# First batch's tiles in the memory of weight steps 12 to 14, weight conversion through the wo ring, and the third batch's pooling tied to weight step 13

## The chip, the cores and the metric

The program runs on one core of one Trainium2 chip. The metric is the device time of one execution in microseconds (us). Before the change the median of three runs is 1892.75 us (1891.44 to 1893.3).

## The reference

What is computed, cut to what matters:

```python
k_p = k.reshape(B, H, Sp, 8, D).mean(axis=3)         # B, H, S, D = 8, 8, 576, 64; Sp = 72
v_p = v.reshape(B, H, Sp, 8, D).mean(axis=3)
attn = softmax(q @ k_p.T / 8)
x = (attn @ v_p)                                     # to (8, 576, 512)
h = x.T @ U @ V                                      # mixing over the 576 tokens, rank 32
u = x + h.T
x1 = u + relu(u @ w_ch1) @ w_ch2                     # 512 -> 2048 -> 512
u2 = x1 + real(fft2(x1))
y = u2 + relu(layernorm(u2) @ w2_ch1) @ w2_ch2
```

The weights, U and V come as float64 and are turned into float32 on the chip, from the two 32-bit words of each number. A product at full precision is made of products of a high part (float32 rounded to the matmul's short form) and a low part (the rest).

## The kernel before

**Weights.** The first layer's two matrices are cut into 16 steps of 128 hidden units. A step has two raw tiles of 512 KB, one for each matrix (`wraw`, loaded at L167 on the SP queue). `w_first` (L159) is the generator that converts a step: `high` makes the top bits in ScalarE (L144, or VectorE at L146 when its last argument is false) and the scaled high word in ScalarE (L147), `bits` joins them with two VectorE operations (L151, L152) into a temporary, and `split` (L107) writes the high part in ScalarE (L108) and the low part in GpSimd (L102) into the weight tile `W[k, f]`. So a step is four operations of 128x512 each on VectorE, four plus two on ScalarE and two on GpSimd. The weight tile takes the memory of its own raw tile: both have the tag `w{k}_{f}`.

**Temporaries before.** The weight tiles' memory is lent out before a step's raw tile arrives: `scratch(i)` (L81) gives tile `w{i % 2}_{15 - i // 2}`. The first batch lives there: five tiles with its queries and its attention output (`xq`, `x0`, scratch 12 to 16, that is the memory of steps 9, 8 and 7), its raw keys and values (scratch 2 to 10), U and V (17 to 19), a table of U (`usf`, scratch 21: step 5), and temporaries of its softmax. A step's raw tiles can be loaded when the lent tile is given back. The conversion's own temporaries are scratch 0 and 1 (the memory of step 15) for steps 0 to 13, one tile for each step in turn, and the two `cv` buffers for steps 14 and 15.

**Attention.** `tile_steps` (L461) does one tile of 128 queries: scores on TensorE, row maxima on VectorE (L486), exponentials on ScalarE (L489), transposes, and the product with the pooled values, scaled by VectorE (L509). `first` (L522) runs the five tiles of batch 0, three at a time, as urgent work; `mix_split` and `mix_mm` (L546, L553) then add the mixing over the tokens, and `block_prep` (L802) transposes and splits the first two blocks of 256 tokens into `utx`. `prep` (L387) loads and pools the keys and values of a batch with nine VectorE reductions (L411, L414) through two `raw` buffers.

**The matmuls of the first layer.** In group 0 blocks 0 and 1 go together through the 16 steps: `st1` (24 matmuls of 256 columns, `h<-utx,w`), then ReLU in ScalarE (L998) and the low part in VectorE (L999), then `st2` (12 matmuls of 512 columns). Later groups take one block each, and the second half of the layer goes through products of combined weights, which `w_combine` (L199) makes: it adds and subtracts converted weights in VectorE through five `wo` buffers and stores them to DRAM. `w_second` (L244) does the second layer's weights through `cv` and `wo`.

**Order.** The program is written as lanes of generators that are stepped in turn. A planner orders each engine's instructions by their place in the program (urgent ones first) and by when its own clock holds them ready, so that late work can stand early in an engine's queue; each engine then runs its queue in that order. Buffers of one tag are handed out in the order of the program. The loads of all kinds share SP's queue.

The lines that gate the raw loads and choose the temporaries:

```python
            while len(raws) < min(NF, upto) and (len(raws) < (NF - 1 if state["free"] else 5) or NF - 2 in ts):
...
                if f < NF - 2:
                    t = scratch(f % 2)
                    t = [t[:, 512 * k:512 * k + 512].bitcast(I32) for k in range(2)]
                else:
                    t = [tmp().bitcast(I32) for k in range(2)]
```

Of the kernel before, what the change touches and what calls it, by code (L numbers as in the profile page):

```python
# [40 lines left out]
NRING = 4  # L41
QAHEAD = 3
# [4 lines left out]
def kernel(  # L47
# [30 lines left out]
    W = {}  # L78
    state = {"n": 0, "free": False, "m": "s1", "u": 0, "slot": 0, "x1": 0, "u2": 0, "op": 0, "clock": 0, "busy": False, "late": None, "tick": 0, "banks": ("s0", "s1", "hu")}
# [79 lines left out]
    def w_first(tmp):  # L159
        raws, ts = {}, {}  # L160

        def loads(upto):
            while len(raws) < min(NF, upto) and (len(raws) < (NF - 1 if state["free"] else 5) or NF - 2 in ts):
                f = len(raws)
                raws[f] = [wp.tile([128, 1024], I32, tag=f"w{k}_{f}", name="wraw") for k in range(2)]
                for k in range(2):
                    nc.sync.dma_start(out=raws[f][k], in_=(w1a, w2a)[k][f].bitcast(I32))  # L167
        def done(f):
            for k in range(2):
                w = wp.tile([128, 2, 512], F32R, tag=f"w{k}_{f}", name="w")  # L170
                W[k, f] = w
                split(w[:, 0], w[:, 1], ts[f][k].bitcast(F32), nc.gpsimd)
        loads(2)
        yield
        for f in range(NF + 1):
            loads(f + 3)
            while len(raws) < min(NF, f + 1):
                yield
                loads(f + 3)
            if f == NF - 1:  # L180
                done(f - 1)
            if f < NF:
                if f < NF - 2:
                    t = scratch(f % 2)
                    t = [t[:, 512 * k:512 * k + 512].bitcast(I32) for k in range(2)]
                else:
                    t = [tmp().bitcast(I32) for k in range(2)]
                ts[f] = t
                for k in range(2):
                    high(raws[f][k], 512, t[k], True)  # L190
            yield
            if f and f != NF - 1:
                done(f - 1)
            if f < NF:
                for k in range(2):
                    bits(raws[f][k], 512, t[k])
                yield
# [132 lines left out]
    class Attn:  # L330
        def __init__(self, c):
# [6 lines left out]
            self.usf = scratch(21)[:, 0:20 * RANK].rearrange("p (t g r) -> p t g r", t=5, g=4)  # L338
# [7 lines left out]
            self.xq = [scratch(12 + t) for t in range(5)]  # L346
# [10 lines left out]
        def tmp(self):  # L357
            return self.p.tile([128, S], F32, tag="raw", name="raw", bufs=2)
# [28 lines left out]
        def prep(self, b):  # L387
# [3 lines left out]
            self.kp[b] = (kp, vp)  # L391

            def load(i):
                t = scratch(2 + i) if b == 0 else self.tmp()
                if i < 4:
                    nc.sync.dma_start(out=t[:, 0:S], in_=kT[b, i])
                else:
                    r0, n = TT[i - 4]
                    nc.sync.dma_start(out=t[:n, 0:512], in_=vr[b, r0:r0 + n, :])
                self.raw[i] = t  # L400
# [60 lines left out]
        def tile_steps(self, b, t, alt=0, before=None):  # L461
# [11 lines left out]
            if 5 * b + t + QAHEAD >= 5:  # L473
                self.q_load(5 * b + t + QAHEAD)
            if before:
                before()
            sf = scratch(3 + alt) if alt else self.s
# [17 lines left out]
            e = scratch(4 + 2 * alt, 640) if alt else p1.tile([128, 640], F32, tag="e", name="e")  # L495
# [635 lines left out]
    lanes["w"] = w_first(at.cv)  # L1131
# [4 lines left out]
    for _ in f:  # L1136
        step("uv")
        step("w")
    with urgent():
        at.mix_split(0)  # L1140
    step("w")
    lanes["prep"] = lane_prep(at)
# [17 lines left out]
    state["free"] = True  # L1160
    hq = []
# [295 lines left out]
```

## Time and profile before

| what | us |
|---|---|
| median of 3 runs | 1892.75 |
| the profiled execution, its own time | 1888.01 |
| span of the profiled execution | 1886.2 |
| TensorE busy in the span | 1821.1 (97%) |
| VectorE busy | 1039.7 (55%) |
| ScalarE busy | 715.7 (38%) |
| GpSimd busy | 194.8 (10%) |

How to read it: the span goes from the first to the last instruction, and all times below are counted from its start. An engine's busy share is an average over stages; TensorE is nearly always busy but in the first part of the span, so the table of stretches below says more than the shares. In a timeline row the bracket at the end is the idle time of the engine before the row and the instruction that ended it.

### The profile page before, as it was taken

How to read it: one execution, taken by the hardware profiler on the slowest of the kernel's cores; microseconds unless marked ns; L12 is line 12 of the kernel's file. 1: busy time of each engine (PE TensorE's matmuls, PEld its weight loads, DVE VectorE, ACT ScalarE, POOL GpSimd, SP SyncE). 2: the span in 40 equal slices, each digit the busy share in tenths (PEclk: the TensorE clock that was granted, in tenths of full speed). 3: DMA queues.
4: the chain of work that ended last, by engine and by line, in shares of the span. 5: the costliest groups of instructions: out<-in, count | busy, mean ns of one | idle time of the engine just before them, and what ended most of it. 6: DMA issues, size and time to landing. Idle time of an engine off the chain costs nothing.

```text
span 1886.2 us, 31833 instructions
## 1 busy us (share of the span) xinstructions
PE 1821.1 (97%) x11492; PEld 1634.8 (87%) x11492; DVE 1039.7 (55%) x2379; ACT 715.7 (38%) x2186; POOL 194.8 (10%) x341
## 2 busy tenths in 40 slices
PE   5789999999999999999999999999999999999999
PEld 3678888888989898899998889899999899989998
DVE  7774575656565544554456655555565444444332
ACT  7672444444434332433324332333333323232321
POOL 3440131222210000000010100000100000000000
PEclk9899999999999999999999999999999999999999
DMA  9754475758575524667677766666676674756563
GB/s 361 255 174 128 144 229 158 244 179 248 164 243 163 176 73 150 220 219 245 216 237 253 276 223 229 227 222 230 225 241 216 213 238 172 238 179 231 182 208 132
DMA packets 265789, 394.41 MB, mean 209 GB/s; under 512 B 61664, under 2 KB 92480, under 8 KB 265632
## 3 DMA queue, kind: packets, MB, share of 16 engines
q1 hardware_dynamic: 264704, 388.97, 62.3%
q0 software_dynamic: 928, 3.40, 0.5%
q8 instruction: 91, 1.49, 0.3%
q14 instruction: 66, 0.54, 0.1%
HBM read 312.73 MB, written 79.56 MB: 208 GB/s over the span
## 4 chain that ended last, share of the span: by engine, by line
PE 62%; DVE 2%; DMA 2%; issue 0%; ACT 0%; SPq 0%; DVEq 0%; ACTq 0%
PE h L112 27%; PE o L112 16%; PE m L112 7%; PE hu L112 7%; PE s L112 4%; PE s L889 1%; DMA w<-wd 0%; DMA R<-x1d 0%; DMA wr<-wc 0%; DMA out<-ur 0%; DMA ur<-u2d 0%; DMA wd<-cv 0%; DVE hl L1278 0%; DVE bs L865 0%; DVE ur L105 0%
## 5 line engine op out<-in xcount | busy, mean ns | idle before, releaser
L112 PEld LDWEIGHTS h<-x,wr 128*128 128x128 f32 x4032 | 527.6, 191 | 24.5 <-DVE side L105 0.8
L112 PE MATMUL h<-x,wr 128*128 128x256 f32 x4032 | 547.9, 284 | 0.2 <-DVE side L105 0.2
L112 PE MATMUL o<-w,hh 128*128 128x512 f32 x1440 | 417.4, 400 | 4.9 <-ACT hh L998 2.5
L112 PE MATMUL h<-utx,w 128*128 128x256 f32 (+1 forms) x2232 | 321.7, 289 | 9.2 <-DVE hl L999 3.8
L112 PEld LDWEIGHTS h<-utx,w 128*128 128x128 f32 x2232 | 301.2, 191 | 29.5 <-DVE hl L999 6.4
L112 PEld LDWEIGHTS o<-w,hh 128*128 128x128 f32 x1440 | 251.0, 190 | 43.5 <-ACT hh L998 5.6
L112 PE MATMUL o<-w,hl 128*128 128x512 f32 x720 | 239.1, 395 | 1.7 <-DVE hl L999 1.7
L105 DVE TENSOR_TENSOR side<-h,side 128x256 f32<-128x256 f32 x192 | 106.3, 554 | 137.8 <-PE h L112 136.9
L112 PEld LDWEIGHTS o<-w,hl 128*128 128x128 f32 x720 | 131.5, 189 | 25.4 <-DVE hl L999 2.1
L1272 ACT ACTIVATE hh<-side 128x256 fp32r<-128x256 f32 x192 | 100.0, 521 | 118.8 <-DVE side L105 112.5
L1272 ACT ACTIVATE hh<-h 128x256 fp32r<-128x256 f32 x96 | 36.8, 383 | 253.2 <-PE h L112 250.8
L1278 DVE SCALAR_TENSOR_TENSOR hl<-h,hh 128x256 fp32r<-128x256 f32 x96 | 40.7, 424 | 158.8 <-ACT hh L1272 158.8
L1278 DVE SCALAR_TENSOR_TENSOR hl<-side,hh 128x256 fp32r<-128x256 f32 x192 | 105.9, 551 | 28.2 <-ACT hh L1272 28.1
L489 ACT ACTIVATE s<-s,mx 128x72 f32<-128x72 f32 x296 | 90.6, 334 | 58.5 <-DVE mx L486 57.5
L112 PE MATMUL m<-w,hh 128*128 128x512 f32 x400 | 109.8, 395 | 0.0
L112 PE MATMUL hu<-w,hh 128*128 128x512 f32 x384 | 104.8, 394 | 0.0
L102 POOL TENSOR_TENSOR wo<-wo 128x256 fp32r<-128x256 f32 x88 | 69.1, 801 | 289.6 <-ACT wo L108 242.8
L998 ACT ACTIVATE hh<-h 128x256 fp32r<-128x256 f32 x158 | 61.4, 389 | 80.5 <-PE h L112 77.8
L999 DVE SCALAR_TENSOR_TENSOR hl<-h,hh 128x256 fp32r<-128x256 f32 x158 | 65.7, 417 | 32.7 <-ACT hh L998 32.1
L102 DVE TENSOR_TENSOR x<-ul,x 128x256 fp32r<-128x256 f32 x154 | 59.3, 421 | 42.2 <-ACT x L108 42.0
L112 PEld LDWEIGHTS m<-w,hh 128*128 128x128 f32 x400 | 69.1, 190 | 9.2
L1317 ACT ACTIVATE side<-h 128x256 f32<-128x256 f32 x96 | 36.7, 383 | 99.4 <-PE h L112 99.4
(252 smaller groups left out, 2390.3 us busy)
## 6 DMA issues: line engine op xcount, KB each, us to landing
wr<-wc SPq DMA_DIRECT2D x336, 512.0 KB
wc<-wo SPq DMA_DIRECT2D x88, 256.0 KB
x<-x SPq DMA_DIRECT2D x56, 256.0 KB
ur<-ud SPq DMA_DIRECT2D x36, 256.0 KB
x1d<-ur SPq DMA_DIRECT2D x36, 256.0 KB
ul<-u2d SPq DMA_DIRECT2D x36, 256.0 KB
ur<-u2d SPq DMA_DIRECT2D x36, 256.0 KB
out<-ur SPq DMA_DIRECT2D x36, 256.0 KB
```

Source lines behind the costliest of these rows:

```text
L102: eng.tensor_tensor(out=o, in0=a, in1=b, op=ALU.subtract)
L105: eng.tensor_tensor(out=o, in0=a, in1=b, op=ALU.add)
L112: nc.tensor.matmul(o, a, b, start=start, stop=stop, skip_group_check=True)
L489: nc.scalar.activation(out=s[:n, a], in_=v[:, k], func=ACTF.Exp, bias=mx[:n, a:a + 1], accum_out=sm[:n, a:a + 1])
L889: nc.tensor.transpose(o[:, k * 128:k * 128 + 128], u[:, k * 128:k * 128 + 128], ident)
L998: nc.scalar.activation(out=hh, in_=p, func=ACTF.Relu)
L999: nc.vector.scalar_tensor_tensor(out=hl, in0=p, scalar=0.0, in1=hh.bitcast(F32), op0=ALU.max, op1=ALU.subtract)
L1272: nc.scalar.activation(out=hh[:, i], in_=c, func=ACTF.Relu)
L1278: nc.vector.scalar_tensor_tensor(out=hl[:, i], in0=c, scalar=0.0, in1=hh[:, i].bitcast(F32), op0=ALU.max, op1=ALU.subtract)
L1317: nc.scalar.activation(out=sb, in_=v, func=ACTF.Copy)
```

## The change

The first batch's five tiles move to scratch 2 to 6 (the memory of steps 14, 13 and 12), its raw keys and values to scratch 7 to 15, `usf` to scratch 16 (step 7), and the softmax's temporaries with them. Raw loads may run to step 11 once the first batch's attention is written, and to step 14 after the first two blocks are prepared. The conversion takes scratch 0 and 1 for steps 0, 1, 4, 5, 8 and 9, and two `wo` buffers each for the other ten steps; it no longer uses `cv`. For steps 0 to 4 the top bits of the first matrix are made in VectorE (L146's form) and no longer in ScalarE. The query loads of batch 1, which were written inside the urgent tiles of batch 0, are written after `mix_split(0)`, with no urgency. In `prep(2)` two small VectorE copies read a part of `W[1, 13]` and write into the tiles of the pooled keys and values.

```diff
+NSCR = 10
 ...
-            while len(raws) < min(NF, upto) and (len(raws) < (NF - 1 if state["free"] else 5) or NF - 2 in ts):
+            while len(raws) < min(NF, upto) and (len(raws) < state["most"] or NSCR + 1 in ts):
 ...
+        def temps(f):
+            if f < NSCR and f % 4 < 2:
+                t = scratch(f % 2)
+                return [t[:, 512 * k:512 * k + 512].bitcast(I32) for k in range(2)]
+            return [tmp().bitcast(I32).rearrange("p h x -> p (h x)") for k in range(2)]
 ...
-            if f == NF - 1:
-                done(f - 1)
             if f < NF:
 ...
-                ts[f] = t
+                ts[f] = temps(f)
                 for k in range(2):
-                    high(raws[f][k], 512, t[k], True)
+                    high(raws[f][k], 512, ts[f][k], k or f >= 5)
             yield
-            if f and f != NF - 1:
+            if f:
                 done(f - 1)
 ...
-            self.usf = scratch(21)[:, 0:20 * RANK].rearrange("p (t g r) -> p t g r", t=5, g=4)
+            self.usf = scratch(16)[:, 0:20 * RANK].rearrange("p (t g r) -> p t g r", t=5, g=4)
-            self.xq = [scratch(12 + t) for t in range(5)]
+            self.xq = [scratch(2 + t) for t in range(5)]
 ...
             self.kp[b] = (kp, vp)
+            if b == 2:
+                for z, i in ((kp, 4), (vp, 5)):
+                    nc.vector.tensor_copy(z[:, :, 0], W[1, NF - 3][:, 0, 0:i].bitcast(F32))
-                t = scratch(2 + i) if b == 0 else self.tmp()
+                t = scratch(7 + i) if b == 0 else self.tmp()
 ...
-            if 5 * b + t + QAHEAD >= 5:
+            if b:
                 self.q_load(5 * b + t + QAHEAD)
-            sf = scratch(3 + alt) if alt else self.s
+            sf = scratch(6 + alt) if alt else self.s
-            e = scratch(4 + 2 * alt, 640) if alt else p1.tile([128, 640], F32, tag="e", name="e")
+            e = scratch(8 + alt, 640) if alt else p1.tile([128, 640], F32, tag="e", name="e")
 ...
-    lanes["w"] = w_first(at.cv)
+    lanes["w"] = w_first(at.wo)
 ...
+    state["most"] = NF - 4
     with urgent():
         at.mix_split(0)
     step("w")
+    for i in range(QAHEAD):
+        at.q_load(5 + i)
 ...
     state["free"] = True
+    state["most"] = NF - 1
```

## Rows read from the trace of the kernel before

**Rows 1.** Busy time by stretch: us, PE, PEld, DVE, ACT, POOL, clock, DMA share, GB/s.

```profile
0.00:62.00 62.00, 31.34 (x146) 23.15 (x146) 50.98 (x95) 45.29 (x147) 23.55 (x36) 0.89 1.01 367
62.00:90.00 28.00, 26.03 (x158) 22.80 (x159) 18.39 (x32) 17.78 (x53) 10.40 (x10) 0.94 0.56 193
90.00:130.00 40.00, 33.69 (x202) 27.56 (x201) 36.19 (x58) 30.60 (x85) 20.80 (x16) 1.00 0.56 177
130.00:188.00 58.00, 54.94 (x353) 49.07 (x352) 25.14 (x51) 19.38 (x70) 4.37 (x7) 1.00 0.46 137
188.00:700.00 512.00, 497.78 (x3200) 449.73 (x3199) 306.34 (x712) 223.39 (x875) 80.82 (x113) 0.99 0.60 185
```

**Rows 2.** Timeline of TensorE, 40 to 68 us: start, duration, instruction, [idle before <-releaser].

```profile
44.87 1.97 PE L112 MATMUL hu<-scr,scr 128*128 128x512 f32 x2 [1.98 <-DVE scr L509]
...
55.19 1.12 PE L812 MATMUL s<-ident,scr 128*128 128x128 f32 x4 [2.67 <-DVE scr L105]
...
62.11 3.15 PE L112 MATMUL h<-utx,w 128*128 128x256 f32 x13 [3.19 <-DVE utx L102]
```

**Rows 3.** Timeline of TensorE, 85 to 130 us.

```profile
98.80 0.74 PE L112 MATMUL o<-w,hl 128*128 128x512 f32 x2 [1.67 <-DVE hl L999]
...
114.83 0.76 PE L112 MATMUL s<-k,q 128*128 128x144 f32 x4 [2.23 <-DVE x L509]
```

**Rows 4.** Timeline of VectorE, 93 to 122 us.

```profile
95.73 2.68 DVE L152 SCALAR_TENSOR_TENSOR scr<-wraw,scr 128x512 int32<-128x512 int32 x1
```

**Rows 5.** Timeline of all engines, 0 to 45 us.

```profile
0.74 1.56 SPq L442 DMA_DIRECT2D q<-qT  x3
...
13.81 2.29 PE L112 MATMUL s<-k,scr 128*128 128x144 f32 x8 [13.81 <-ACT k L421]
```

**Rows 6.** Groups of instructions, 13.8 to 62 us: busy us, mean ns.

```profile
L144 ACT ACTIVATE scr<-wraw 128x512 int32<-128x512 uint32 x13 | 8.8, 720 | 0.0
...
L105 DVE TENSOR_TENSOR wo<-w 128x256 f32<-128x256 f32 x6 | 3.4, 590 | 0.8 <-POOL w L102 0.8
...
L102 DVE TENSOR_TENSOR wo<-wo 128x256 f32<-128x256 f32 x4 | 2.7, 677 | 0.0
```

**Rows 7.** Line 146 over the whole span: ns min/median/max, first and last start.

```profile
L146 DVE TENSOR_SCALAR wo<-cv x32: 277/294/831, 293.6 to 516.7; 128x256 int32<-128x256 int32 x32
```

**Rows 8.** Timeline of VectorE, 41 to 62 us.

```profile
42.72 1.49 DVE L102 TENSOR_TENSOR wo<-wo 128x256 f32<-128x256 f32 x1
...
46.16 0.68 DVE L151 SCALAR_TENSOR_TENSOR scr<-wraw,scr 128x512 int32<-128x512 int32 x1
...
49.99 2.75 DVE L152 SCALAR_TENSOR_TENSOR scr<-wraw,scr 128x512 int32<-128x512 int32 x2
52.66 1.75 DVE L151 SCALAR_TENSOR_TENSOR cv<-wraw,cv 128x512 int32<-128x512 int32 x1
54.45 0.69 DVE L105 TENSOR_TENSOR scr<-o,scr 128x512 f32<-128x512 f32 x1
```

**Rows 9.** Timeline of GpSimd, 40 to 64 us.

```profile
49.22 6.32 POOL L102 TENSOR_TENSOR w<-scr,w 128x512 fp32r<-128x512 f32 x4 [3.87 <-DMA wc<-w]
...
63.04 1.48 POOL L102 TENSOR_TENSOR w<-cv,w 128x512 fp32r<-128x512 f32 x1 [0.83 <-ACT w L108]
```

**Rows 10.** Timeline of SP's queue, 116 to 140 us: first load of the second layer's weights.

```profile
131.56 0.64 SPq L248 DMA_DIRECT2D cv<-w1b  x1
```

**Rows 11.** Groups of instructions on VectorE, 90 to 130 us.

```profile
L414 DVE TENSOR_REDUCE vp<-raw 128x64 f32<-128x512 f32 (+1 forms) x8 | 5.3, 668 | 0.0
...
L411 DVE TENSOR_REDUCE kp<-raw 128x72 f32<-128x576 f32 x4 | 3.0, 738 | 0.0
```

**Rows 12.** Timelines of GpSimd, TensorE and ScalarE: last conversion, 16th step, batch 2's keys.

```profile
137.56 1.29 POOL L102 TENSOR_TENSOR w<-cv,w 128x512 fp32r<-128x512 f32 x1 [6.61 <-ACT w L108]
...
181.24 3.14 PE L112 MATMUL h<-utx,w 128*128 128x256 f32 x24
...
148.06 0.90 ACT L421 ACTIVATE k<-kp 64x288 f32<-64x288 f32 x2 [2.02 <-PE s L112]
```

More of the change, by code (lines that the diff above doesn't have):

```diff
@@ L78 @@
     W = {}
-    state = {"n": 0, "free": False, "m": "s1", "u": 0, "slot": 0, "x1": 0, "u2": 0, "op": 0, "clock": 0, "busy": False, "late": None, "tick": 0, "banks": ("s0", "s1", "hu")}
+    state = {"n": 0, "free": False, "m": "s1", "u": 0, "slot": 0, "x1": 0, "u2": 0, "op": 0, "clock": 0, "most": 5, "busy": False, "late": None, "tick": 0, "banks": ("s0", "s1", "hu")}
     def scratch(i, w=1024, dt=F32):
@@ L179, in w_first @@
                 loads(f + 3)
-            if f == NF - 1:
-                done(f - 1)
             if f < NF:
[L183 to L187, printed above, removed]
-                ts[f] = t
+                ts[f] = temps(f)
                 for k in range(2):
-                    high(raws[f][k], 512, t[k], True)
+                    high(raws[f][k], 512, ts[f][k], k or f >= 5)
             yield
-            if f and f != NF - 1:
+            if f:
                 done(f - 1)
@@ L195, in w_first @@
                 for k in range(2):
-                    bits(raws[f][k], 512, t[k])
+                    bits(raws[f][k], 512, ts[f][k])
                 yield
```

## The prediction

> **What bounds the kernel now.** I read the table of stretches first. From 188 us on TensorE is busy for 497.8 of 512 us, and for 54.9 of 58 us in the stretch before; up to 62 us it is busy for 31.3 us alone, and from 90 to 130 us for 33.7 of 40 [rows 1]. TensorE's work is not changed by this change, so what can be won is its idle time: 30.7 us before 62, 2.0 us from 62 to 90, 6.3 us from 90 to 130 and 3.1 us from 130 to 188. What is saved there moves all that follows forward, since TensorE stays the bound.
>
> Then the waits that open these gaps. Before the first matmul of the first layer (62.11 us) TensorE waits for VectorE again and again: 1.98, 2.67 and 3.19 us [rows 2]. From 90 to 130 us it is VectorE again, 1.67 and 2.23 us for a low part and for an attention tile [rows 3]. VectorE is busy for 51.0 of the first 62 us and for 36.2 of the 40 us [rows 1]. What stands before these late results in its queue is conversion: a joining step took 2.68 us at 95.73, and the low part that TensorE waited for came next [rows 4]. So the bound of both stretches is VectorE's queue, in order, with ScalarE close behind (45.3 of 62, 30.6 of 40 us).
>
> **The change part by part.** Durations are from the profiled execution, 1888.01 us, whose span is 1886.2 us; the median of the runs shown is 4.7 us above it, and I take the sum off the median. A minus is time saved.
>
> *Query loads.* Three loads of batch 1's queries stand first in SP's queue, for 1.56 us, ahead of the keys whose pooling the first matmul (13.81 us) waits for [rows 5]. They lose their urgency and go behind. The issue alone gives 1.6 us; as transfers they are 0.79 MB, 2.1 us at the 367 GB/s of that stretch [rows 1]. If V and U, on another queue, hold the keys back instead, little is left, say 0.5. I take -1.6, the time of the row itself. Their new place is behind the early raw loads; batch 1's first tile needs them only after the first layer has begun (62.11 us now), so no one waits there.
>
> *Top bits from ScalarE to VectorE.* One conversion takes 0.72 us on ScalarE [rows 6]. Five move; three belong to steps 0 to 2 and stand between the exponentials, so up to 2.2 us of ScalarE's part of the chain goes. The place may be filled by the next conversion; between 0 and -2.2 I take -1.0, a little under half. On VectorE the nearest row has 256 columns at 0.294 us [rows 7], so 512 are at most 0.59, five 2.9 us. Not all stand ahead of an urgent instruction: between 0 and +2.9 I take +1.2.
>
> *Temporaries in wo.* The ten VectorE operations of w_combine that the planner drew into this stretch cost 3.4 and 2.7 us, together 6.1 [rows 6]. One of them, 1.49 us long, stood directly before the result behind TensorE's 1.98 us wait [rows 2, 8]. The `wo` buffers now go to the steps' temporaries first, so the adds must come behind the conversion. That buffers are handed out in program order shows in `cv`: GpSimd was done with both buffers of step 14 at 64.52, yet the second layer's first load, which needs nothing else, was only issued at 131.56, after step 15 had had its turn [rows 9, 10]. Between -1.5 (that one) and -6.1 I take -3.0, since conversion fills a part of the room. Later the adds meet a VectorE that is busy for 306 of 512 us: no cost; without that slack their 6.1 us would come back.
>
> *Pooling of batch 2.* Of the rows from 90 to 130 us four reductions of keys (738 ns) and five of the eight of values (668 ns) are batch 2's, 6.3 us [rows 11]. They leave the crowded stretch for the time after step 13's conversion. TensorE idles 6.3 us in it, but most of a wait is a joining step, and one reduction stood ahead of about half the waits: between -0.7 (one reduction) and -6.3 I take -3.0. The two copies themselves are a few columns wide. They wait in VectorE's queue for step 13's high part, with low parts and row maxima queued behind: between 0 and 2 us (a wait like the largest in rows 3), I take +0.5.
>
> *Memory and ring.* Raw tiles of steps 5 to 11 may come earlier, those of 12 to 14 only once the first batch's tiles are stored, as 7 to 9 do now. The ring is two steps deeper. Neither is on TensorE's path now: the last conversion starts at 137.56 and the 16th step's matmuls at 181.24 [rows 12]. So I take 0, between -3 (the 2.0 and 1 us of small gaps from 62 to 90 and after 130) and +4: one more step's four joining steps, at the 0.68 us of the free case [rows 8] with GpSimd's collisions on top, ahead of the urgent chain.
>
> Sum: -1.6 - 1.0 + 1.2 - 3.0 - 3.0 + 0.5 + 0 = -6.9 us; 1892.75 - 6.9 = 1885.9 us. All low ends together give -20, all high ends +6.
>
> **Rule beside row.** While GpSimd's four subtractions ran from 49.22 to 55.54, three joining steps of 0.68 us took 2.75 and 1.75, so the urgent addition came at 54.45 and TensorE's next work at 55.19 [rows 2, 8, 9]. The Trainium skill (SBUF — State Buffer, "Who interferes with whom") says that a VectorE instruction with two SBUF inputs and a GpSimd instruction that reads SBUF exclude each other, and that the second waits for the whole of the first. By that rule the deeper ring is a danger, since it brings more subtractions beside joining steps into the early stretch; the rows above agree. What it could make of the time is the first rival's sum; with no further collisions the sum above stands.
>
> **The rivals.**
> 1. *Slower: conversion crowds the urgent chain (0.13).* Now the early conversion runs dry: a part of step 5's memory holds the table of U, which the sum that ends at 46.84 us still reads [rows 2]. With that memory free, two more steps could enter the queue from 44 to 62 us. That is eight joining steps, 5.4 us free, plus twice the 2.5 us that four subtractions cost (4.5 instead of 2.0): 10.4 us. If the stretch from 62 to 90 also idles like the next one (6.3 us in 40, so 4.4 in 28 instead of 2.0), 2.4 more. 12.8 - 6.9 gives +5.9, 1898.7 us. It decides from 10.7 us of delay on. For: the rows above. Against: VectorE is already full there, and the planner puts urgent work first.
> 2. *Absorbed (0.2).* ScalarE and VectorE stay full, freed room is refilled with conversion, and only the start's 1.6 us and one reduction's 0.7 remain: 1890.4 us. For: VectorE has no free room up to 62 us.
> 3. *All of it (0.2).* The adds' 6.1, the reductions' 6.3, the start's 1.6 and ScalarE's 2.2 come through whole: -16.2, 1876.6 us. For: each sat in a full in-order queue. Against: the longest waits were behind joining steps.
> 4. *The adds do not leave (0.06).* If w_combine still comes early, its term falls: -3.9, 1888.9 us. Against: the cv row.
> 5. *Batch 2 comes late (0.06).* Its keys are needed at 148.06 [rows 12]. If its pooling starts only with the last conversion at 137.6, nine reductions (6.3 us) and seven loads behind two buffers (256 KB at the 177 GB/s of rows 1, 1.5 us each) end near 154; a score matmul at the head of TensorE's queue would stand for 6 us: 6 - 6.9, 1891.9 us. Against: TensorE has first-layer work to 188.
>
> **How the numbers follow.** The forecast has 0.35, with a range of its own from 1882 to 1889. A measurement of this kernel can tell 0.2% from no change, that is 3.8 us: faster is below 1889.0, slower above 1896.5. Faster: most of the forecast (0.33), rival 3 (0.2), half of rival 4 and a quarter of rival 2 (0.08): 0.61. Slower: rival 1 and a little of 2 and 5: 0.15. Same: the rest, 0.24. The range reaches from rival 3 to beyond 2 and 5, 1875 to 1896; outside are rival 1 and the far ends.
>
> **What would show it.** In the new profile: the first matmul near 12.2 us instead of 13.8; the first layer's first matmul at 57 to 59 us instead of 62.1; no VectorE `wo<-w` before the last conversion; no pooling of batch 2 before step 13; TensorE's idle time from 90 to 130 us at about 3 us instead of 6.3. Wrong would be a first-layer start at 62 us or later, or VectorE waits in front of TensorE as long as now, with as many joining steps over 1 us.

## The result, and the profile after

The changed kernel takes 1902.76 us (median of 4 runs, 1900.58 to 1906.19), the kernel before 1892.1 us (4 runs) on the same chip: a ratio of 1.0051, 95% interval 1.0039 to 1.0063, so 10.7 us slower. I had forecast 1885.9 us, 6.9 us faster. The profiled execution of the changed kernel took 1900.69 us, its span is 1898.9 us. Lines of the code have moved down by one to three: the matmul helper is now L113, the top bits L145 and L147, the joining operations L152 and L153, the split L109 and L103.

The table of stretches of the changed kernel, with the columns of [rows 1]:

```profile
0.00:62.00 62.00, 35.31 (x159) 28.03 (x160) 52.44 (x93) 44.38 (x145) 26.51 (x38) 0.83 1.02 370
62.00:90.00 28.00, 22.31 (x127) 18.43 (x126) 21.57 (x36) 23.15 (x63) 14.67 (x12) 0.94 0.81 274
90.00:130.00 40.00, 31.01 (x170) 25.98 (x170) 33.74 (x55) 20.89 (x53) 16.42 (x13) 0.91 0.44 132
130.00:188.00 58.00, 56.43 (x365) 50.72 (x364) 24.09 (x49) 19.65 (x76) 2.13 (x5) 1.00 0.35 107
188.00:700.00 512.00, 493.23 (x3157) 442.92 (x3156) 304.00 (x711) 223.21 (x877) 81.27 (x113) 0.99 0.60 185
```

Read it against [rows 1]. From 62 to 90 us TensorE is busy for 22.31 us instead of 26.03, from 90 to 130 us for 31.01 instead of 33.69, and there the mean granted clock is 0.91 instead of 1.00. The conversion has run ahead: in 62 to 90 us ScalarE is busy for 23.15 instead of 17.78 us and the DMA moves 274 instead of 193 GB/s. Of the 64 joining operations of VectorE, 48 have started by 90 us, where 38 had before.

**Where the time went.** TensorE's work is the same, so a span is its work plus its idle time, plus what it loses at half clock. I counted, from the matmul and clock records, the idle time plus half of the time that TensorE was busy at half clock. What is left of the span is 1812.2 us before and 1813.0 us after, so this loss explains nearly all of the difference of the spans (12.7 us):

| loss of TensorE, us | 0 to 62 | 62 to 130 | 130 to 255 | 255 to 710 | after 710 | sum |
|---|---|---|---|---|---|---|
| before | 34.6 | 9.9 | 7.8 | 12.9 | 8.9 | 74.0 |
| changed | 33.9 | 19.5 | 7.6 | 16.1 | 8.9 | 85.9 |

So 9.6 us come from 62 to 130 us: 6.4 us of idle time (by the rows above and [rows 1], as stretch less busy time: 5.69 + 8.99 against 1.97 + 6.31) and 3.2 us of half clock. Another 3.2 us come from 255 to 710 us. Over the whole span idle time rose from 65.1 to 70.6 us and the loss at half clock from 8.9 to 15.4 us: more than half of the 11.9 us is half clock. Up to 62 us idle time fell by 4.0 us, and 3.3 of them came back as half clock.

What TensorE waited for from 62 to 130 us (total us, times, longest), first in the kernel before:

```profile
PE h L112 <- DVE utx L102: 3.7, 2, 3.2
PE s L112 <- DVE x L509: 2.2, 1, 2.2
PE o L112 <- DVE hl L999: 1.7, 1, 1.7
PE h L112 <- ACT hh L998: 1.4, 2, 0.8
PE o L112 <- ACT hh L998: 1.3, 2, 0.7
```

and in the changed kernel:

```profile
PE o L113 <- ACT hw L1001: 3.3, 2, 2.5
PE hu L113 <- DVE xl L103: 3.0, 1, 3.0
PE o L113 <- ACT hh L1001: 2.0, 2, 1.3
PE o L113 <- DVE hl L1002: 1.6, 2, 1.0
PE h L113 <- DVE hl L1002: 1.6, 1, 1.6
PE h L113 <- ACT hw L1001: 1.6, 1, 1.6
```

The waits behind ScalarE have grown from 2.7 to 6.9 us, and their longest was for `hw` (the high part of a result), for which ScalarE made TensorE wait nowhere in this stretch before. One of them, in the timelines of ScalarE and TensorE of the changed kernel:

```profile
74.58 2.95 ACT L145 ACTIVATE wo<-wraw 128x512 int32<-128x512 uint32 x5
77.37 0.43 ACT L1001 ACTIVATE hw<-h 128x256 fp32r<-128x256 f32 x1
```

```profile
77.86 0.73 PE L113 MATMUL h<-w,hw 128*128 128x512 f32 x2 [1.57 <-ACT hw L1001]
...
79.61 4.52 PE L113 MATMUL h<-utx,w 128*128 128x256 f32 x24 [0.55 <-DVE hw L1002]
```

Five top-bit conversions in a row, into `wo` tiles of the ring, now stand ahead of `hw`. In the kernel before ScalarE did at most two such conversions (L144) in a row from 62 to 100 us, into the one tile of a step.

The longest of these waits has another origin. ScalarE's row, then TensorE's:

```profile
109.00 0.63 ACT L109 ACTIVATE w<-wo 128x512 fp32r<-128x512 f32 x1 [3.21 <-DVE wo L153]
```

```profile
110.53 2.07 PE L113 MATMUL o<-w,hw 128*128 128x512 f32 x4 [2.48 <-ACT hw L1001]
```

ScalarE, with `hw` next but one in its queue (110.09 us), itself stood 3.21 us for a joining operation, and that one stood on VectorE behind the tie's copy of 2.85 us (shown under e8).

The longest wait of the crowded stretch, VectorE's timeline and then TensorE's:

```profile
114.13 1.86 DVE L106 TENSOR_TENSOR wo<-w 128x256 f32<-128x256 f32 x2
115.91 0.68 DVE L153 SCALAR_TENSOR_TENSOR wo<-wraw,wo 128x512 int32<-128x512 int32 x1
116.51 0.74 DVE L414 TENSOR_REDUCE kp<-raw 128x72 f32<-128x576 f32 x1
117.17 0.41 DVE L103 TENSOR_TENSOR wo<-wo 128x256 f32<-128x256 f32 x1
117.50 0.74 DVE L414 TENSOR_REDUCE kp<-raw 128x72 f32<-128x576 f32 x1
118.16 1.08 DVE L103 TENSOR_TENSOR xl<-x,xh 128x512 fp32r<-128x512 f32 x1
```

```profile
119.30 0.50 PE L113 MATMUL hu<-xl,ust 128*128 128x512 f32 x1 [2.99 <-DVE xl L103]
...
120.36 3.90 PE L113 MATMUL h<-utx,w 128*128 128x256 f32 x18 [0.56 <-DVE hw L1002]
```

The high part of this tile was there at 114.53, so `xl` could have begun then. In front of it stood three additions and subtractions of w_combine, two reductions of batch 2 and one joining operation: but for the last, the very work that my two largest terms had sent out of the early and the crowded stretch.

The start did what was forecast, and then lost it (TensorE, then VectorE):

```profile
10.78 2.29 PE L113 MATMUL s<-k,scr 128*128 128x144 f32 x8 [10.78 <-ACT k L424]
...
44.46 2.08 PE L113 MATMUL hu<-scr,scr 128*128 128x512 f32 x2 [4.25 <-DVE scr L512]
...
60.35 1.82 PE L113 MATMUL h<-utx,w 128*128 128x256 f32 x13 [1.61 <-DVE utx L103]
```

```profile
39.19 2.37 DVE L153 SCALAR_TENSOR_TENSOR wo<-wraw,wo 128x512 int32<-128x512 int32 x2
41.48 1.40 DVE L414 TENSOR_REDUCE kp<-raw 128x72 f32<-128x576 f32 x2
```

The first matmul comes 3.0 us earlier than in [rows 5]. But the same sum that began at 44.87 after 1.98 us of waiting [rows 2] now begins at 44.46 after 4.25: joining operations and batch 1's pooling took the room. The first layer begins 1.8 us earlier, at 60.35 us: later than the 57 to 59 that I had named as a sign of being right, and before the 62 that was to show me wrong.

### The profile page after: what moved, and what is told of

The parts are those of the page before. It is cut to its first block, busy times and chain, and to the rows that moved or that the text cites. A ratio compares the mean times of both kernels' runs of the same rounds, so it can differ in the third digit from the quotient of the medians.

```text
span 1898.9 us, 31848 instructions
## 1 busy us (share of the span) xinstructions
PE 1828.4 (96%) x11492; PEld 1639.5 (86%) x11492; DVE 1041.9 (55%) x2386; ACT 714.7 (38%) x2181; POOL 196.1 (10%) x341
## 4 chain that ended last, share of the span: by engine, by line
PE 68%; DMA 5%; DVE 3%; issue 1%; ACT 1%; SPq 0%; POOL 0%; DVEq 0%; ACTq 0%
PE h L113 29%; PE o L113 19%; PE hu L113 7%; PE m L113 7%; PE s L113 5%; PE s L892 1%; DMA wc<-wo 1%; DMA ud<-x 1%; DMA x<-x 1%; DMA ul<-ud 1%; DMA wd<-cv 0%; DMA raw<-vr 0%; DMA cv<-w1b 0%; DMA R<-x1d 0%; DMA w<-wd 0%
## 5 line engine op out<-in xcount | busy, mean ns | idle before, releaser
L113 PEld LDWEIGHTS h<-x,wr 128*128 128x128 f32 x4032 | 527.4, 191 | 24.7 <-DVE side L106 1.0
L113 PE MATMUL h<-x,wr 128*128 128x256 f32 x4032 | 547.7, 283 | 0.2 <-DVE side L106 0.2
L113 PE MATMUL o<-w,hh 128*128 128x512 f32 x1440 | 417.4, 400 | 5.3 <-ACT hh L1001 3.8
L113 PE MATMUL h<-utx,w 128*128 128x256 f32 (+1 forms) x2232 | 325.9, 291 | 10.8 <-DVE hl L1002 6.5
L113 PEld LDWEIGHTS h<-utx,w 128*128 128x128 f32 x2232 | 305.6, 193 | 32.9 <-DVE hl L1002 9.8
L113 PEld LDWEIGHTS o<-w,hh 128*128 128x128 f32 x1440 | 250.6, 190 | 43.8 <-ACT hh L1001 6.8
L113 PE MATMUL o<-w,hl 128*128 128x512 f32 x720 | 239.0, 395 | 1.6 <-DVE hl L1002 1.6
L113 PEld LDWEIGHTS o<-w,hl 128*128 128x128 f32 x720 | 131.1, 189 | 26.1 <-DVE hl L1002 2.8
L113 PE MATMUL m<-w,hh 128*128 128x512 f32 x400 | 109.8, 394 | 0.0
L113 PE MATMUL hu<-w,hh 128*128 128x512 f32 x384 | 104.7, 394 | 0.0
L103 POOL TENSOR_TENSOR wo<-wo 128x256 fp32r<-128x256 f32 x88 | 69.4, 805 | 290.9 <-ACT wo L109 235.8
L103 DVE TENSOR_TENSOR x<-ul,x 128x256 fp32r<-128x256 f32 x154 | 59.2, 420 | 42.5 <-ACT x L109 42.4
L113 PEld LDWEIGHTS m<-w,hh 128*128 128x128 f32 x400 | 69.1, 190 | 9.3
```

The lines of the kernel that those rows point to most:

```text
L103: eng.tensor_tensor(out=o, in0=a, in1=b, op=ALU.subtract)
L113: nc.tensor.matmul(o, a, b, start=start, stop=stop, skip_group_check=True)
```

## The experiments

The theories, as the expectations name them. **A**: the wo ring lets conversion run ahead and crowd the urgent work; A1 says that it does so by itself, A2 only with the early raw tiles. **B**: the tie's two copies cost. **C**: the planner makes a new order of any edit, and the order by itself moves the time by several us. **D**: the early raw tiles alone cost. **E**: GpSimd's subtractions hold VectorE operations that stand on the path. Every run has its own runs of the kernel before beside it, on the same chip; "loss" below is the sum of the table above, in the run's profiled execution.

### Parts taken out of the changed kernel

**No tie** (e1):

```diff
-            if b == 2:
-                for z, i in ((kp, 4), (vp, 5)):
-                    nc.vector.tensor_copy(z[:, :, 0], W[1, NF - 3][:, 0, 0:i].bitcast(F32))
```

> The changed kernel without the two copies that tie batch 2's pooling to step 13. Theory A (the ring): conversion through wo puts runs of up to five conversions in ScalarE's queue ahead of the ReLUs, TensorE idles and its clock falls; the copies matter little: 1900 to 1904 us, as changed (1902.8). Theory B (the tie): the copy that took 2.85 us in VectorE at 105.5 us, with the 2.48 us that TensorE then idled and the 3.4 us at half clock behind it, is the main loss: 1895 to 1898 us. Theory C (any new order of the queues moves the time by some us): anywhere from 1893 to 1906.

Measured: 1899.09 us, before 1892.69; ratio 1.0036 [1.0020, 1.0051]. The interval overlaps that of the whole change. The tie may be worth 3 us, and most of the loss stays: 18.6 us from 62 to 130. The time lies between the ranges of A and B.

**Tie on ScalarE** (e8):

```diff
-                    nc.vector.tensor_copy(z[:, :, 0], W[1, NF - 3][:, 0, 0:i].bitcast(F32))
+                    nc.scalar.activation(out=z[:, :, 0], in_=W[1, NF - 3][:, 0, 0:i].bitcast(F32), func=ACTF.Copy)
```

> The changed kernel with the two tying copies on ScalarE in place of VectorE: the same dependence, without VectorE's meeting with GpSimd. Theory B in its narrow form (the copy is held up by a GpSimd subtraction): the 2.85 us wait is gone, 1896 to 1899 us, near the kernel without the tie. Theory A: 1900 to 1904 us.

Measured: 1898.48 us, before 1892.69; ratio 1.0030 [1.0020, 1.0040]. In the changed kernel one copy of four columns took 2.85 us, while GpSimd's subtractions followed each other. VectorE, then GpSimd:

```profile
105.53 2.85 DVE L394 COPY kp<-w 128x4 f32<-128x4 f32 x1
```

```profile
105.80 2.55 POOL L103 TENSOR_TENSOR w<-wo,w 128x512 fp32r<-128x512 f32 x2
```

With the copies gone from VectorE, the next joining operation was held in the same place:

```profile
105.49 3.19 DVE L153 SCALAR_TENSOR_TENSOR wo<-wraw,wo 128x512 int32<-128x512 int32 x1
```

So the copy's 2.85 us are not the copy's own price. The runs below without GpSimd's subtractions confirm it: the same copy takes 0.15 to 0.17 us in all three of them that have the tie (e10, e16, e21), and 0.66 to 4.10 us in four other kernels that have it on VectorE beside the subtractions (e2, e3, e7b, e13).

**Old temporaries** (e2):

```diff
...
-            if f < NSCR and f % 4 < 2:
+            if f < NF - 2:
...
-    lanes["w"] = w_first(at.wo)
+    lanes["w"] = w_first(at.cv)
```

> The changed kernel with the conversion's temporaries as before (scratch 0 and 1 in turn, cv for the last two steps); the memory, the tie, the shifts and the query loads stay changed. Theory A: the loss goes, since at most two steps are in flight: TensorE's idle time from 62 to 130 us back from 14.7 to about 9 us, 1890 to 1895 us. Theory B: the copies still wait, 1899 to 1904 us. Theory C: no ordered answer.

Measured: 1895.16 us, before 1892.69; ratio 1.0009 [0.9999, 1.0020]; the loss from 62 to 130 us is 12.4 instead of 19.5. By itself this says that the ring is the cause. It didn't last: see the controls. 45 of the 64 joining operations had started by 90 us here, nearly as many as in the changed kernel.

**All top bits on ScalarE** (e3):

```diff
-                    high(raws[f][k], 512, ts[f][k], k or f >= 5)
+                    high(raws[f][k], 512, ts[f][k], True)
```

> The changed kernel with all top bits of the first weight's slabs taken on ScalarE again. By the prediction's two terms (1.0 off ScalarE, 1.2 on VectorE) nothing is left of it: 1902.5 with 1.5 either way. Rival: on VectorE they stand ahead of urgent work in a queue that is full, so without them the time falls by 3 or more, to 1899 or below. Second rival: ScalarE's runs of conversions get longer, hw and hh come later, and the time rises by 3 or more, to 1906.

Measured: 1905.77 us, before 1892.55; ratio 1.0071 [1.0056, 1.0086], 3 us above the whole change with intervals that overlap. There is no sign that the operations moved to VectorE cost.

### Parts of the change alone, on the kernel before

**The ring** (e9):

```diff
...
-                if f < NF - 2:
+                if f < 10 and f % 4 < 2:
...
-    lanes["w"] = w_first(at.cv)
+    lanes["w"] = w_first(at.wo)
```

> The kernel before with the wo ring alone (steps 2, 3, 6, 7 and 10 to 15 through wo, the rest in scratch 0 and 1); memory, pooling, shifts and query loads as before. Theory A1 (the ring by itself lets conversions pile up in front of the ReLUs): 1897 to 1903 us, with TensorE's idle time from 62 to 130 us above 11 us (8.3 before). Theory A2 (the ring hurts only with the new memory, since before raw tiles of steps 5 to 9 came too late for it): 1890 to 1894 us.

Measured: 1906.07 us, before 1893.46; ratio 1.0065 [1.0052, 1.0079]. The ring alone is slower than the whole change, and than A1's range. Its conversion does not run ahead: 36 joining operations had started by 90 us, 38 before. Its stretch from 90 to 130 us:

```profile
90.00:130.00 40.00, 25.43 (x115) 20.21 (x115) 40.00 (x55) 28.34 (x71) 24.61 (x17) 0.78 0.64 192
```

VectorE is busy for all of the 40 us (36.19 in [rows 1]) and TensorE for 25.43. Its longest waits there were for split tiles and low parts behind VectorE's queue (two more, 1.86 and 2.14 us, for the masked values `v` that GpSimd makes):

```profile
109.69 0.80 PE L112 MATMUL hu<-xl,ust 128*128 128x512 f32 x1 [3.33 <-DVE xl L102]
...
128.98 0.89 PE L112 MATMUL o<-w,hw 128*128 128x512 f32 x2 [2.83 <-DVE hw L997]
```

**The memory** (e6): the changed kernel with the old temporaries, no tie, all top bits on ScalarE and the query loads urgent again, so that the new places of batch 0's tiles and the loads that they let through are left.

> The changed kernel with the memory's new place alone: old temporaries, no tie, all top bits in ScalarE, urgent query loads. Theory A2: with at most two steps in flight the early raw tiles do no harm, 1889 to 1894 us. Theory D (early raw tiles alone crowd the stretch from 62 to 90 us): 1896 to 1902 us with more than 42 of the 64 joining steps done at 90 us (38 before, 48 as changed).

Measured: 1897.27 us, before 1893.46; ratio 1.0026 [1.0015, 1.0036]. 45 joining operations had started by 90 us. By this run theory D stands for 3.8 us, in this one order.

**The late query loads** (e5):

```diff
-            if 5 * b + t + QAHEAD >= 5:
+            if b:
                 self.q_load(5 * b + t + QAHEAD)
...
+    for i in range(QAHEAD):
+        at.q_load(5 + i)
```

> The kernel before, with the change's late query loads alone (three loads behind the first layer instead of ahead of it). By the prediction's term the first matmul comes 3 us earlier (10.8 instead of 13.8) and the end 1.6 us: 1890.5. Theory C (the planner's order after that decides): first matmul near 10.8 all the same, but the first-layer start anywhere from 59 to 66 and the end anywhere from 1885 to 1900, with the gain of the start not found again at the end. If the ring and the order it makes are what costs in the changed kernel, this kernel isn't above 1896.

Measured: 1891.27 us, before 1892.55; ratio 0.9994 [0.9985, 1.0004]. The first matmul comes at 9.70 us, 4.1 us earlier, and 1.3 us are left, not told from none.

### Controls: the same work in another order

**Swap of two loads, kernel before** (e7), **changed kernel** (e7b) and **changed kernel with old temporaries** (e13). A step's two raw tiles are loaded in the other order, nothing else:

```diff
-                for k in range(2):
+                for k in (1, 0):
                     nc.sync.dma_start(out=raws[f][k], in_=(w1a, w2a)[k][f].bitcast(I32))
```

> The kernel before, with the two raw loads of a step issued in the other order: an edit with no purpose, to see what a mere reordering by the planner does. Theory C: it differs from before (1892.1) by more than 3 us. Theories A and B: within 2 us of before.

Measured: 1899.05 us, before 1892.69; ratio 1.0036 [1.0022, 1.0051]. Nothing but the order has changed, and 6.4 us are lost. The trace shows one place, batch 1's scores, which the planner now put ahead of the first layer's matmuls on TensorE:

```profile
69.38 1.33 PE L112 MATMUL s<-k,q 128*128 128x144 f32 x4 [6.73 <-ACT k L421]
70.85 4.39 PE L112 MATMUL h<-utx,w 128*128 128x256 f32 x24
```

> The changed kernel with w2's slab loaded ahead of w1's: the same work, another order. Theory A: 1903 with 4 either way, 8 above the one with the old temporaries and the same swap. Theory C: anywhere from 1893 to 1910, and it may lie below the one with the old temporaries.

> The changed kernel with the old temporaries (as in the run that has them) and, besides, w2's slab loaded ahead of w1's, which alone is neutral work in another order. Theory A (the ring costs 8 us by itself): about as the one with the old temporaries, 1895 with 4 either way, and some 8 below the changed kernel with the same swap. Theory C (any new order moves the time by several us): anywhere from 1888 to 1908, with no fixed distance to the changed kernel with the same swap.

Measured, both beside 1892.55 for before: the changed kernel with the swap 1903.10 us, ratio 1.0053 [1.0038, 1.0067]; with the swap and the old temporaries 1904.43 us, ratio 1.0063 [1.0044, 1.0083]. So the ring's price read in one order (1902.76 against 1895.16, 7.6 us) is gone in the other (1903.10 against 1904.43). Theory A as "the ring costs 8 us" falls. What stands is that three of the four kernels of this family lie near 1903 us and one does not: theory C has a part.

### Without GpSimd's subtractions

**Zeros for the low parts**, in the changed kernel (e10), the kernel before (e11), the ring alone (e14), the swap alone (e15) and the changed kernel with the swap (e16):

```diff
-                split(w[:, 0], w[:, 1], ts[f][k].bitcast(F32), nc.gpsimd)
+                nc.scalar.activation(out=w[:, 0], in_=ts[f][k].bitcast(F32), func=ACTF.Copy)
+                nc.gpsimd.memset(w[:, 1].bitcast(F32), 0.0)
```

> The changed kernel with GpSimd's subtraction, which makes the low part of each weight of w_first, replaced by a GpSimd memset of that part to zero: the low parts are left out. It keeps an operation of GpSimd there that writes and does not read. Theory E (the joining steps' meetings with GpSimd's reads make the loss): no joining step over 1 us, and the time falls by 8 us or more against the changed kernel, to the level of the kernel before with the same edit. Theory A (the number of conversions in the queues, not their collisions): it falls by 2 to 6 us and stays 5 us or more above the kernel before with the same edit.

> The kernel before with the same edit, low parts of w_first's weights left out, a GpSimd memset in place of each subtraction. 14 of its 64 joining steps took over 1 us and the 64 lost 11 us together; those on TensorE's path are a part: both theories expect 1882 to 1890 us.

> The kernel before with the wo ring alone, and GpSimd's subtraction in the first weight's conversion replaced by a write of zeros (the low parts of the first weight's slabs are left out). The ring alone cost 12 us beside before. Theory E (the ring's order costs because more VectorE operations wait for GpSimd's subtractions): the cost goes, 1883 to 1888, and TensorE's idle time plus half of its half-clock time in 62 to 130 us comes near the 7.8 of the kernel before with the same edit. Theory C (the order as such, queues standing in each other's way): it stays, 1892 to 1897, with 15 us or more there.

> The kernel before with w2's slab loaded ahead of w1's (that alone cost 7 us) and the same write of zeros for the subtraction (low parts of the first weight's slabs left out). Theory E: the cost goes, 1883 to 1887. Theory C: it stays, 1889 to 1893; what was seen in that order, batch 1's first scores ahead of the first layer's first matmuls on TensorE's queue, has nothing to do with GpSimd, so of the swap's loss I expect more than half to stay.

> The changed kernel with w2's slab first and the same write of zeros (low parts of the first weight's slabs left out). Theory E: as the changed kernel with that edit, 1887 with 3 either way, 15 below the one with the subtractions. Theory C: the orders stay apart, 1892 or more, or below 1883.

Measured, as medians with the distance to the kernel before in the same column (for the left column to its own runs beside each):

| order | with the subtractions | with zeros | ratio of the one with zeros to the kernel before |
|---|---|---|---|
| before | 1892.1 to 1893.5 | 1883.40 | 0.9949 [0.9936, 0.9962] |
| swap alone | 1899.05 (+6.4) | 1888.53 (+5.1) | 0.9978 [0.9969, 0.9987] |
| ring alone | 1906.07 (+12.6) | 1890.67 (+7.3) | 0.9989 [0.9980, 0.9998] |
| changed | 1902.76 (+10.7) | 1887.49 (+4.1) | 0.9972 [0.9958, 0.9987] |
| changed, swap | 1903.10 (+10.5) | 1889.31 (+5.9) | 0.9978 [0.9969, 0.9988] |

Every order gains 9 to 15 us, and the four distances fall from 10 us in the mean to 5.6. So in these kernels somewhat under half of the distance goes with GpSimd's subtractions, and the rest stays with the order. Two things limit this: the four distances share one kernel of reference, and the edit itself gives the planner new work to order. I had expected theory E to take nearly all of the ring's 12 us; 7.3 stayed. For the swap more than half stayed, as expected. The loss from 62 to 130 us speaks for E more clearly: with the subtractions it is 9.9 us before and 19.2 to 24.9 in the four other orders, with zeros 7.8 and 10.5 to 12.2.

VectorE's two groups of joining operations into `wo` from 62 to 130 us (busy us, mean ns) in the changed kernel:

```profile
L153 DVE SCALAR_TENSOR_TENSOR wo<-wraw,wo 128x512 int32<-128x512 int32 x16 | 13.5, 874 | 0.0
L152 DVE SCALAR_TENSOR_TENSOR wo<-wraw,wo 128x512 int32<-128x512 int32 x15 | 11.8, 810 | 1.6 <-ACT wo L145 1.4
```

and with zeros written in place of the subtractions:

```profile
L153 DVE SCALAR_TENSOR_TENSOR wo<-wraw,wo 128x512 int32<-128x512 int32 x14 | 9.4, 704 | 0.5 <-ACT wraw L148 0.4
L152 DVE SCALAR_TENSOR_TENSOR wo<-wraw,wo 128x512 int32<-128x512 int32 x14 | 9.3, 706 | 2.1 <-ACT wo L145 2.0
```

Over all 64 joining operations, what lies above 0.69 us each sums to 11.2 us in the changed kernel and to 0.6 us with zeros. The Trainium skill (SBUF — State Buffer, "Who interferes with whom") says that a VectorE instruction with two SBUF inputs contends with a GpSimd instruction that reads SBUF, and not with one that only writes it; these rows agree with both halves.

The number of held microseconds does not by itself make a kernel slow. They are 11.1 us before, 11.2 after and 11.3 with the swap alone; the ring alone has 17.7 and the late query loads, no slower than before, 12.4. That it depends on which instruction stands behind a held one fits the wait at 110.53, but no run shows it apart from the order.

**The subtractions on VectorE**, nothing left out, in the kernel before (e18), the changed kernel (e21), and the kernel before with the late query loads (e19):

```diff
-                split(w[:, 0], w[:, 1], ts[f][k].bitcast(F32), nc.gpsimd)
+                split(w[:, 0], w[:, 1], ts[f][k].bitcast(F32))
```

> The kernel before with the first weight's subtractions on VectorE instead of GpSimd: nothing left out. 32 operations of 0.68 us come onto VectorE (22 us), and the 11 us by which its 64 joining operations were above 0.69 go, as does the GpSimd latency of 1.3 to 1.7 us each. Theory E with a VectorE that has the room: faster, 1884 to 1890. Rival: VectorE, which was busy 36.2 of 40 us in 90 to 130, is now the bound of that stretch and the weights come later: 1897 or more.

Measured: 1891.56 us, before 1893.30; ratio 0.9991 [0.9982, 1.0000]. At best a little faster, and in neither range of the expectation.

> The changed kernel with the first weight's 32 subtractions on VectorE, nothing left out. Theory E: the half of the loss that came from operations held by GpSimd's subtractions goes, 1893 to 1897, and no VectorE operation of the conversion takes over 1.2 us. Rival: 22 us more work on VectorE and a changed order cost as much as they free: 1900 or more.

Measured: 1895.29 us, before 1892.84; ratio 1.0012 [1.0003, 1.0020], so the changed kernel's 10.7 us become 2.5. To the kernel before with the same edit it is 0.21%, 4 us, the same distance that is left with zeros. The conversion's three groups from 62 to 130 us:

```profile
L103 DVE TENSOR_TENSOR w<-wo,w 128x512 fp32r<-128x512 f32 x16 | 10.8, 690 | 0.0
L152 DVE SCALAR_TENSOR_TENSOR wo<-wraw,wo 128x512 int32<-128x512 int32 x14 | 9.5, 710 | 0.6 <-ACT wo L145 0.6
L153 DVE SCALAR_TENSOR_TENSOR wo<-wraw,wo 128x512 int32<-128x512 int32 x14 | 9.2, 678 | 0.0
```

A joining operation takes 0.67 us in the mean (18.7 for 28) instead of 0.82 (25.3 for 31), and 10.8 us of subtractions come on top. VectorE is busier in the stretch, 58.5 instead of 55.3 us, and the program is still 7 us faster.

But it was not won where E says. From 62 to 130 us the loss is 19.8 us, as large as in the changed kernel (19.5); from 130 to 255 us it is 1.5 instead of 7.6, and the changed kernel's last subtraction of this conversion had ended at 118.70. In the crowded stretch the holding has turned round. GpSimd's row and TensorE's, then VectorE's copy that had taken 2.85 us:

```profile
95.81 3.45 POOL L434 TENSOR_SCALAR v<-vp 64x64 f32<-64x64 f32 x1 [5.27 <-DVE vp L417]
```

```profile
99.31 0.69 PE L113 MATMUL s<-v,e 128*128 128x64 f32 x2 [3.93 <-POOL v L434]
```

```profile
98.29 0.15 DVE L394 COPY kp<-w 128x4 f32<-128x4 f32 x1
```

The same GpSimd operation took 0.80 us in the changed kernel (105.03 us). Here it took 3.45, while VectorE ran subtractions and joining operations one behind the other, and TensorE waited 3.93 us for its result.

> The kernel before with late query loads (alone 1.3 us below) and the subtractions on VectorE (alone 1.7 us below). If the two add up: 1889 to 1891, below both kernels. If the order decides (theory C): anywhere from 1885 to 1899.

Measured: 1893.63 us, before 1892.84; ratio 0.9999 [0.9990, 1.0009]. The two small distances don't add up. None of the complete kernels is below the kernel before by more than the measurement can tell.

**The whole set.** In all but one of the 20 profiled executions the span less the loss lies between 1809.9 and 1813.5 us (the kernel before with the subtractions on VectorE has 1817.2), so the loss accounts for their differences. Up to 62 us it is 33.1 to 36.2 us in every complete kernel, whether the first matmul comes at 9.70 or at 15.01 us. The stretch from 62 to 130 us differs most, 9.9 us before, 12.4 with the old temporaries, 24.9 with the ring alone.

## Why the prediction was wrong

**The step that failed** is "Memory and ring", which I took as 0 because "neither is on TensorE's path now". The ring alone measured +12.6 us and the memory alone +3.8, where I had bounded the two at +4 together. The reason I gave looked at when the last weights are needed (181.24 us [rows 12]). What it left out is what stands ahead of other work in the in-order queues: five conversions on ScalarE ahead of `hw`, late work on VectorE ahead of `xl`, and, with the ring alone, a VectorE that is busy for all of the 40 us from 90 on. That conversion runs ahead is not enough by itself: ten more joining operations by 90 us come with the new memory (45 with it and the old temporaries, at 1895.16 us), and the ring alone lost most with 36. The controls add that the size of this isn't a property of the ring: in another order of the same work it was 1.3 us the other way. So the step fails by what was measured, and what sets the size stays open.

**A term that the sum did not have** is TensorE's half clock: I wrote that what can be won is its idle time. In the profiles 6.5 of the 11.9 us lost are half clock, and 3.3 of the 4.0 us of idle time won up to 62 us went back into it.

**The first rival** had the sign, and about half the size (+5.9, 1898.7 us), and I gave it 0.13. It was right in part by luck: I put 10.4 us of delay before 62 us, where nothing was lost, by more held time on VectorE, which over the whole conversion did not grow (11.1 and 11.2 us); and 2.4 us into 62 to 90 us, where idle time rose from 1.97 to 5.69. My argument against it, that the planner puts urgent work first, holds for the start alone: the program marks as urgent only the first batch's work up to the first two blocks. `hw` and batch 1's `xl` are not marked, and late joining operations, additions and reductions stand before `xl` at 114 to 118 us.

**Query loads (-1.6).** The first matmul came 3.0 us earlier, more than forecast, and alone these loads gave 1.3 us, not told from none. So the place was right, and a gain of this size is neither shown nor excluded; in the changed kernel VectorE's queue took 1.2 of the 3.0 us back before the first layer.

**Top bits (-1.0 + 1.2).** On VectorE five of them took 3.1 us (2.3 and 0.8 in the groups of 13.8 to 62 us), a little over the bound of 2.9. With all of them on ScalarE the time rises by 3 us, with intervals that overlap: nothing here speaks against a sum of about 0, and a gain isn't shown.

**Adds leave (-3.0), pooling of batch 2 leaves (-3.0).** The first left the place that I named and came to a worse one, the second never left. The additions and subtractions ran from 111.92 us on, inside 90 to 130 us: 4.9 us of them (groups of 3.3 and 1.6). Pooling there took 8.3 us in twelve reductions (L414 3.0, L417 4.0 and 1.3), as in [rows 11]. Nine of the twelve are batch 2's, all of them. Step 13 came sooner: its last joining operation began at 99.82 us instead of 116.82. It goes with the new memory (105.93 us with the memory alone, 103.20 with the old temporaries in the changed kernel, 117.03 with the ring alone). So tying the pooling to it sent it nowhere. The step assumed step 13 at its old time while another term moved it; and even at the old time, with the high part written by 118.16 us, the pooling would have begun inside the stretch.

**Copies (+0.5).** One took 2.85 us and the other 0.59. This time belongs to GpSimd's subtractions: with the copies on ScalarE a joining operation took 3.19 us in that place, and where GpSimd does no subtractions the copies take 0.15 to 0.17 us.

**The sum as a whole** added terms of 1 to 3 us as if the order of all other work stayed. A swap of two loads, with no term at all, measured 6.4 us. Against that, a term of 3 us read from one trace has no sign.

**What is settled and what is open.** Settled: 9.6 of the 11.9 us lost sit in TensorE's waits from 62 to 130 us and in the half clock that follows them; a joining operation or a small copy beside GpSimd's subtractions takes up to 4.10 us, and without them at most 1.00 and 0.17; and an edit that changes only the order can move the time by 6.4 us. Both edits that take the subtractions away bring the changed kernel to 4 us from the kernel before with the same edit. With zeros the loss from 62 to 130 us has shrunk; with the subtractions on VectorE it has not. Not settled: whether the subtractions cost by holding VectorE or also by their own 1.3 to 1.7 us on the way to the weight, since both edits take away both, and how much of what they won is a new order, since both edits make one; and what makes the kernel before's order 5 us better than four others, when another new order (the late query loads) is as fast as it.

## What to carry to other kernels

Where a planner orders the queues, a part of a change can't be priced from one kernel with it and one without: make the same work run in a second order (swap two loads that don't depend on each other) and see how much of the effect is left; one more order is the least, and says nothing of how wide the orders spread. Work that is "not on the path" is free only while something holds it back; when a change lets it run ahead, look at what stands behind it in each in-order queue before calling it 0. And when two terms of a sum meet in one stretch (an earlier step 13, and work tied to step 13), work them out together.

## What the hardware showed that I had not expected

The half clock. Stretches of the changed kernel at the two levels (columns of [rows 1]):

```profile
69.30:72.30 3.00, 3.00 (x26) 3.00 (x25) 2.36 (x5) 3.00 (x16) 0.00 (x0) 1.00 0.88 273
79.60:82.70 3.10, 3.09 (x14) 3.09 (x15) 3.10 (x6) 3.10 (x13) 0.30 (x1) 0.50 1.03 416
```

The granted clock is 1.00 (2.4 GHz) in the one and 0.50 (1.2 GHz) in the other. The 24 matmuls of a step took 3.02 us at 69.27 and 4.52 us at 79.61, after TensorE had waited in pieces of 0.83, 1.57 and 0.55 us. In the changed kernel this happened three times from 75 to 130 us, in the kernel before not once in that stretch. So short waits can cost half as much again: 1.5 us behind waits that sum to 3.0.

And a VectorE copy of four columns took 2.85 us, through two GpSimd subtractions (105.80 to 108.35) that followed each other. It did not slip in between them; it ended when the second did. In the changed kernel with the swap it took 4.10 us, and where GpSimd did no subtractions 0.15 to 0.17.
